# Modulation columns with 64 moving columns in place of one, and refitted order constants, in an adaLN attention and MLP block

## The chip, the cores and the metric

The kernel runs on one core of one Trainium2 chip. The metric is the device time of one execution in microseconds (us). Every time is that of the slowest core, here the only one. A single core has no die to be compared with, so a run counts as fast unless it is over 1.5% above the fastest of its kernel.

The engines are called by the names of the profile: PE is TensorE, PEld its weight loads, DVE is VectorE, ACT is ScalarE, POOL is GpSimd. SP is SyncE, which here only issues DMA transfers, one after the other, in a fixed order.

## The reference, cut to what matters

```python
B, S, D, H = 1, 2048, 640, 32          # Dh = 20, F = 1536, all bf16
mod = (silu(c) @ w_mod).reshape(1, 6, 1, 640)
sa, ca, ga, sb, cb, gb = ...           # six rows of 640
h = layernorm(x) * (1 + ca) + sa
q, k, v = heads(h @ wqkv)
x = x + ga * (softmax(q @ k.T * Dh**-0.5) @ v) @ wo
h = layernorm(x) * (1 + cb) + sb
x = x + gb * ((h @ w_gate) * (h @ w_up)) @ w_down
```

Four of the six modulation vectors (sa, ca, sb, cb) are needed as columns, with the 640 features on partitions. The kernel makes them with thin matmuls: a 128x128 block of w_mod is the stationary operand, and one column of silu(c) is the moving one. They are 25 matmuls to a vector, 100 in all. Two vectors are made at the start, two between 76 and 83 us.

## The kernel before

A scheduler in the kernel file simulates all engines when the kernel is built. It writes out one fixed order of instructions for each engine. It has a model of TensorE's clock, with a constant of 3413.3 ns (HAM_W), and where that model asks for it, it puts in "fillers" (identity matmuls of 512 columns). So each constant below changes the order of instructions and not the clock itself. Of the clock: from the first clock record (6.11 us in before) to the end of the span it is 1.00 but for two stretches at 0.50, of 3.41 and 10.24 us in before. The two starts lie 20 times 3.41 us apart in before. A window is below such a stretch of 3.41 us, at either clock.

```python
STEAL_GAP = 300.0       # ScalarE may take over VectorE's copies before 60 us if it is idle this long
HAM_W = 3413.3
CHUNKS = [(0, 512), (512, 512), (1024, 512), (1536, 256), (1792, 256)]   # query columns
QUADS = [(1, 2, 2, 3, 2, 3, 2, 3), 3, 3, (1, 1, 2, 1, 1, 1, 1, 1), (1, 1, 1, 1, 1, 0, 0, 0)]
```

The work of attention goes through 5 chunks of queries times 8 items (one item is 4 heads). ScalarE makes most exponentials. A "quad" is four 512-column units whose exponential VectorE approximates with shifted terms; QUADS says how many quads each item has. A tuple lists the eight items of a chunk, a number stands for all eight.

The column round:

```python
C512, C320, C128, C1 = 216.0, 136.0, 57.0, 26.0        # ns in the scheduler's model

def col_round(v, slot, prio, plus):
    dm, buf = d_wm[v]
    mms = []
    for nbk in range(KD):                               # KD = 5 blocks of 128
        for k in range(KD):
            f = lambda e, b, nbk=nbk, k=k: e.matmul(
                ps[:, b, nbk:nbk + 1], buf[:, k, nbk * 128:(nbk + 1) * 128],
                scol[:, k:k + 1], start=(k == 0), stop=(k == KD - 1))
            mms.append((C1, f))
    # ... then one VectorE copy of ps[:, b, 0:KD] to mcol[:, slot, :]
```

K and Q take a way through DRAM: TensorE makes them, VectorE or ScalarE copies them to the buffer KPA, SyncE writes them to k_rows and q_rows, and SyncE loads them again in the layout that the scores need. All these transfers stand in SyncE's one queue.

The softmax here doesn't subtract the row's maximum and nothing guards it: scores larger than these inputs give would overflow.

## Time and profile before

| | before |
|---|---|
| time, median of 3 runs | 869.32 us (866.98 to 870.48) |
| profiled execution | 867.68 us, span of the trace 865.9 us |
| mean granted clock | 0.992 |
| last exponential on ScalarE ends | 829.00 us |

The first row of the page gives the busy time of each engine, its share of the span and its count of instructions. Lower on the page, one row gives the shares of the chain of work that ended last.

```profile
PE 829.4 (96%) x13568; PEld 327.5 (38%) x13568; DVE 713.1 (82%) x1338; ACT 802.5 (93%) x718; POOL 32.0 (4%) x65
...
PE 44%; ACT 34%; DVE 15%; issue 3%; DMA 2%; POOL 1%; SPq 1%; DVEq 0%; ACTq 0%
```

TensorE and ScalarE are both nearly full, and the chain passes back and forth between them. A shares row like this cannot tell what a change in one stage is worth. This is the timeline of SyncE before (start, length, queue, line, operation, destination and source, count), which I read only afterwards:

```profile
79.53 5.06 SPq L970 DMA_DIRECT2D KT<-k_rows  x8
84.64 0.42 SPq L957 DMA_DIRECT2D k_rows<-KPA  x1
85.20 0.34 SPq L979 DMA_DIRECT2D QT<-q_rows  x1
```

The load of QT for item 2 is issued at 85.20 us, behind eight KT loads. The semaphore that tells of its landing has its last increment at 87.88 us. The score matmuls that need it start at 89.22 us:

```profile
88.30 0.98 PE L747 MATMUL ps_all<-wmb,SCb 128*32 128x320 bf16 x24
89.22 0.60 PE L1180 MATMUL ps_all<-QT,KT 32*128 32x512 bf16 x6
```

The trace shows no wait there, because TensorE came late after three windows at half clock (0.50 from 77.80 to 88.04 us).

### The profile page before, as it was taken

The numbers are of one execution on the slowest core, as the hardware profiler recorded it, in microseconds if no ns is written. First come the engines' busy times: TensorE is split into PE (matmuls) and PEld (weight loads), VectorE is DVE, ScalarE is ACT, GpSimd is POOL, SyncE is SP. The second block draws the span as 40 slices with busy tenths as digits, with TensorE's granted clock in tenths as the row PEclk, the third lists the DMA queues.
The fourth block names the chain that finished last, engine by engine and source line by source line (L and its number), as shares of the span: only waits on it lengthen the run. The fifth ranks groups of instructions, "written<-read, shape, count | busy, mean of one in ns | idle before, by whom it ended". The sixth has DMA issues, their size and how long they took to land.

```text
span 865.9 us, 30616 instructions
## 1 busy us (share of the span) xinstructions
PE 829.4 (96%) x13568; PEld 327.5 (38%) x13568; DVE 713.1 (82%) x1338; ACT 802.5 (93%) x718; POOL 32.0 (4%) x65
## 2 busy tenths in 40 slices
PE   8899999999999999999999999999999999999998
PEld 4433333322233322233333322223445444455577
DVE  7865888796999999999889999999779877775463
ACT  4698999999999999899999999999999999999931
POOL 2300000000001000000000100000001100000000
PEclk9997999999999999999999999999999999999999
DMA  9163331122510125110301011110310036203640
GB/s 300 38 216 94 92 86 37 29 71 76 156 29 23 33 55 146 43 24 6 66 10 44 5 36 44 44 36 2 67 50 7 21 75 139 59 21 82 136 88 18
DMA packets 118459, 56.37 MB, mean 65 GB/s; under 512 B 84439, under 2 KB 118327, under 8 KB 118327
## 3 DMA queue, kind: packets, MB, share of 16 engines
q1 hardware_dynamic: 117399, 53.26, 24.2%
q8 instruction: 107, 1.75, 0.9%
q10 hardware_dynamic: 928, 1.15, 0.4%
q14 instruction: 25, 0.20, 0.1%
HBM read 42.93 MB, written 9.16 MB: 60 GB/s over the span
## 4 chain that ended last, share of the span: by engine, by line
PE 44%; ACT 34%; DVE 15%; issue 3%; DMA 2%; POOL 1%; SPq 1%; DVEq 0%; ACTq 0%
ACT PP L1214 34%; PE ps_all L747 16%; PE ps_all L1596 13%; PE ps_all L1180 12%; DVE DB L1238 4%; DVE DSS L1252 3%; PE ps_all L914 2%; DVE st L802 1%; DMA k_rows<-KPA 1%; DVE st L1400 1%; DVE xck L1390 1%; DVE OT L1305 1%; DVE xn L1407 1%; PE ps_all L829 1%; DMA stg<-in_B_w_gate_dram 1%
## 5 line engine op out<-in xcount | busy, mean ns | idle before, releaser
L1214 ACT ACTIVATE PP<-ps_all 128x1536 bf16<-128x1536 f32 (+1 forms) x691 | 788.3, 1279 | 13.5 <-PE ps_all L1180 9.7
L1180 PE MATMUL ps_all<-QT,KT 32*128 32x512 bf16 (+1 forms) x2560 | 295.2, 341 | 14.5 <-ACT PP L1214 11.5
L1252 DVE TENSOR_SCALAR DSS<-DB 128x2048 int16<-128x2048 int16 x400 | 265.9, 683 | 20.0 <-PE ps_all L1596 17.7
L1238 DVE TENSOR_SCALAR DB<-ps_all 128x512 int16<-128x512 f32 x320 | 217.2, 682 | 38.7 <-PE ps_all L1180 37.0
L1180 PEld LDWEIGHTS ps_all<-QT,KT 32*128 32x128 bf16 x2560 | 77.2, 91 | 256.6 <-ACT PP L1214 185.7
L1596 PE MATMUL ps_all<-PP,Vf 128*32 128x512 bf16 (+3 forms) x2184 | 171.9, 344 | 1.5 <-DVE OT L1305 1.5
L1596 PE MATMUL ps_all<-DSS,Vf 128*32 128x512 bf16 (+2 forms) x1880 | 151.7, 351 | 0.0
L747 PE MATMUL ps_all<-h2T,stg 128*32 128x512 bf16 x1440 | 109.7, 381 | 2.8 <-DVE DB L1238 1.7
L1596 PEld LDWEIGHTS ps_all<-PP,Vf 128*32 128x32 bf16 (+1 forms) x2184 | 48.3, 94 | 95.3 <-issue 84.9
L1596 PEld LDWEIGHTS ps_all<-DSS,Vf 128*32 128x32 bf16 (+1 forms) x1880 | 47.8, 96 | 36.1 <-issue 16.0
L747 PE MATMUL ps_all<-wd,hprod 128*32 128x320 bf16 x1152 | 55.2, 300 | 0.4 <-DVE DB L1238 0.3
L747 PEld LDWEIGHTS ps_all<-h2T,stg 128*32 128x32 bf16 x1440 | 34.8, 96 | 35.1 <-issue 9.4
L1465 DVE CAST gsb<-ps_all 128x512 bf16<-128x512 f32 (+1 forms) x48 | 29.5, 615 | 10.8 <-PE ps_all L747 10.6
L747 PEld LDWEIGHTS ps_all<-wd,hprod 128*32 128x32 bf16 x1152 | 29.2, 96 | 14.9 <-issue 4.8
L747 PE MATMUL ps_all<-wV,hT 128*32 128x320 bf16 x640 | 32.9, 300 | 1.9 <-DVE DB L1238 0.8
L1403 POOL TENSOR_SCALAR sd<-mv 128x1 f32<-128x1 f32 x14 | 7.0, 499 | 739.7 <-DVE mv L1402 739.7
L747 PE MATMUL ps_all<-wo,Ocp 128*32 128x320 bf16 x640 | 31.9, 300 | 0.4 <-DVE xck L1390 0.3
L1596 PE MATMUL ps_all<-DB,Vf 128*32 128x512 bf16 (+2 forms) x376 | 32.1, 349 | 0.0
L1305 DVE STREAM_TRANSPOSE OT<-ps_all 128x512 f32<-128x512 f32 (+1 forms) x40 | 24.2, 605 | 8.8 <-PE ps_all L1596 8.6
L914 PE MATMUL ps_all<-hT,wk 128*32 128x512 bf16 x380 | 29.9, 381 | 0.4 <-DVE Vf L994 0.4
L914 PE MATMUL ps_all<-hT,wq 128*32 128x512 bf16 x375 | 29.0, 394 | 0.9 <-DVE Vf L994 0.3
L1476 DVE TENSOR_TENSOR hprod<-ps_all,gsb 128x512 bf16<-128x512 f32 x36 | 24.5, 681 | 5.3 <-PE ps_all L747 5.3
(107 smaller groups left out, 486.6 us busy)
## 6 DMA issues: line engine op xcount, KB each, us to landing
stg<-in_B_w_gate_dram SPq DMA_DIRECT2D x50, 160.0 KB
stg<-in_B_w_up_dram SPq DMA_DIRECT2D x50, 160.0 KB
KT<-k_rows SPq DMA_DIRECT2D x120, 32.0 KB
QT<-q_rows SPq DMA_DIRECT2D x22, 128.0 KB
wm<-in_w_mod_dram SPq DMA_DIRECT2D x3, 800.0 KB
k_rows<-KPA SPq DMA_DIRECT2D x18, 128.0 KB
x<-in_A_x_dram SPq DMA_DIRECT2D x7, 320.0 KB
xck<-in_A_x_dram SPq DMA_DIRECT2D x3, 640.0 KB
```

The lines of the kernel that those rows point to most:

```text
L747: return lambda e, b: e.matmul(ps[32 * x:32 * x + 32, b, 0:n], lhs()[:, 32 * x:32 * x + 32], rhs(), tile_position=(0, 32 * x), start=st, s ...
L802: bns.append(dve(393, lambda e, t=t, i=i, hf=hf: e.bn_stats(st[:, i, 6 * hf:6 * hf + 6], x0[:, t, 320 * hf:320 * hf + 320]), [d_x[tc][i // ...
L829: f = lambda e, b, i=i, k=k: e.transpose(bankh(b)[:, i * 128:(i + 1) * 128], xn[:, s2, i, k * 128:(k + 1) * 128], ident[:])
L914: f = [lambda e, b_, k=k, x=x: e.matmul(ps[x:x + min(32, w - x), b_, :], wx[:, k, r0 + x:r0 + min(x + 32, w)], hT[tc][:, k, :], tile_posit ...
L1180: ems.append(lambda e, i=i, kt=kt: e.matmul(dstf()[:, i * u.n:(i + 1) * u.n], KT[32 * u.s:32 * u.s + 32, u.j, kt * 128:(kt + 1) * 128], QT ...
L1214: return e.activation(PPs[g % 2][:, cellp["p"], 0:nu * 512], ps[:, b0:b0 + nu, :].rearrange("p b c -> p (b c)"), AFT.Exp, scale=ESCALE)
L1238: return e.tensor_scalar(DB0[:, st_["slot"], x * 512:(x + 1) * 512], bank(cell["b"]), EBIAS, 0.0, op0=ALU.add, op1=ALU.max)
L1252: return e.tensor_scalar(DSS[:, cell["s"], :], DB0[:, st_["slot"], :], float(SHIFTS[jj]), None, op0=ALU.add)
L1305: t1 = Task("dve", n * 1.1 + 70, lambda e: e.transpose(OT[:, 0:n], ps[:, BPV, 0:n]), [], prio=0.0, name=f"T1.{it}")
L1465: f = lambda e: e.tensor_copy(gsb[:, gs, 0:n], ps[:, r.b["b"], 0:n])
L1476: f = lambda e: e.tensor_tensor(hprod[:, fc, 0:n], ps[:, r.b["b"], 0:n], gsb[:, gs, 0:n], ALU.mult)
L1596: ems.append(lambda e, i=i, kt=kt, stt=stt, stp=stp: e.matmul(ps[32 * s:32 * s + mc, BPV, 0:u.n], Vf[:, (kt * H + 4 * u.j + s) * VW:(kt * ...
```

## The change

The intent: each thin matmul takes the same column of silu(c) repeated 64 times as its moving operand, so that TensorE has more work where its clock had fallen to 0.50 (77.80 to 88.04 us of before), at little cost in time. The scheduler's model is told so, it drops fillers, and the constants of the order are chosen anew. The whole of it:

```diff
-STEAL_GAP = 300.0
+STEAL_GAP = 200.0
-QUADS = [(1, 2, 2, 3, 2, 3, 2, 3), 3, 3, (1, 1, 2, 1, 1, 1, 1, 1), (1, 1, 1, 1, 1, 0, 0, 0)]
+QUADS = [(1, 2, 2, 3, 3, 3, 3, 3), 3, 3, 1, (1, 0, 1, 0, 1, 0, 1, 0)]
-    C512, C320, C128, C1 = 216.0, 136.0, 57.0, 26.0
+    C512, C320, C128, C1 = 216.0, 136.0, 57.0, 28.0
+    NCOL = 64
-                f = lambda ...: e.matmul(ps[:, b, nbk:nbk + 1], buf[:, k, nbk * 128:(nbk + 1) * 128],
-                                         scol[:, k:k + 1], ...)
+                f = lambda ...: e.matmul(ps[:, b, nbk * NCOL:nbk * NCOL + NCOL],
+                                         buf[:, k, nbk * 128:(nbk + 1) * 128],
+                                         scol[:, k:k + 1].to_broadcast([128, NCOL]), ...)
+        def src(r):        # the copies read one column of each 64
+            return ps[:, r.b["b"], 0:KD * NCOL].rearrange("p (a b) -> p a b", b=NCOL)[:, :, 0]
-            sc.activity(start, 1.0 if cand.name[:3] == "col" else cand.dur * 2.37)
+            sc.activity(start, cand.dur * 2.37)
```

There are 80 quads before and after. Chunk 0 has two more (items 4 and 6), chunks 3 and 4 have one less each. The fillers in the order go from 48 to 36.

More of the change, by code (lines that the diff above doesn't have):

```diff
@@ L760, in col_round @@
             for k in range(KD):
-                f = lambda e, b, nbk=nbk, k=k: e.matmul(ps[:, b, nbk:nbk + 1], buf[:, k, nbk * 128:(nbk + 1) * 128],
-                                                        scol[:, k:k + 1], start=(k == 0), stop=(k == KD - 1))
+                f = lambda e, b, nbk=nbk, k=k: e.matmul(ps[:, b, nbk * NCOL:nbk * NCOL + NCOL],
+                                                        buf[:, k, nbk * 128:(nbk + 1) * 128],
+                                                        scol[:, k:k + 1].to_broadcast([128, NCOL]),
+                                                        start=(k == 0), stop=(k == KD - 1))
                 mms.append((C1, f))
+        def src(r):
+            return ps[:, r.b["b"], 0:KD * NCOL].rearrange("p (a b) -> p a b", b=NCOL)[:, :, 0]
         def after(r):
             if plus:
-                f = lambda e: e.tensor_scalar(mcol[:, slot, :], ps[:, r.b["b"], 0:KD], 1.0, None, op0=ALU.add)
+                f = lambda e: e.tensor_scalar(mcol[:, slot, :], src(r), 1.0, None, op0=ALU.add)
             else:
-                f = lambda e: e.tensor_copy(mcol[:, slot, :], ps[:, r.b["b"], 0:KD])
+                f = lambda e: e.tensor_copy(mcol[:, slot, :], src(r))
             return [dve(75, f, [r.last], prio=0)]
```

## The prediction

> **What bounds the kernel now.** I read the page first: TensorE is 96% busy and ScalarE 93%, and the chain that ended last is shared between them (PE 44%, ACT 34%). Then the table of busy time by stretches, to see which of the two binds where:
>
> ```profile
> 80.00:90.00 10.00, 10.00 (x135) 3.90 (x136) 1.65 (x6) 6.21 (x6) 0.00 (x0) 0.60 0.46 112
> ...
> 100.00:150.00 50.00, 48.04 (x698) 15.96 (x694) 42.12 (x73) 49.91 (x46) 0.00 (x0) 1.00 0.26 67
> ```
>
> Columns: PE, PEld, DVE, ACT, POOL busy, then granted clock, DMA share, GB/s. From 90 us on ScalarE (the exponentials, L1214) is busy all the time: it binds until its last exponential at 829 us, with TensorE close behind; after it TensorE alone finishes in 34 us. In 80-90 us ScalarE works only 6.21 of 10 us and the granted clock is 0.60. So the page's row of PEclk is next; it has two dips, at the start and here:
>
> ```profile
> PEclk9997999999999999999999999999999999999999
> ```
>
> Finer stretches put the edges of half clock at 9.52 to 12.93 us and 77.80 to 88.04 us: one and three times 3.41 us, and the two starts are 20 times 3.41 us apart. So the clock is decided on a fixed grid of 3.41 us. On that grid:
>
> ```profile
> 74.39:77.80 3.41, 2.10 (x37) 0.94 (x34) 1.89 (x3) 2.60 (x3) 0.00 (x0) 1.00 0.24 62
> 77.80:81.21 3.41, 3.41 (x38) 1.02 (x37) 0.69 (x1) 2.38 (x2) 0.00 (x0) 0.50 0.50 119
> 81.21:84.63 3.42, 3.42 (x46) 1.38 (x43) 0.33 (x2) 2.46 (x3) 0.00 (x0) 0.50 0.44 105
> 84.63:88.04 3.41, 3.41 (x33) 0.95 (x33) 0.69 (x1) 2.34 (x2) 0.00 (x0) 0.50 0.39 107
> 88.04:91.45 3.41, 3.19 (x57) 1.32 (x49) 2.04 (x4) 1.93 (x3) 0.00 (x0) 1.00 0.30 80
> ```
>
> The timeline of TensorE shows what stood in the window before the drop, and in the next ones: the modulation columns (L761, one moving column each) and an idle gap of 1.31 us.
>
> ```profile
> 75.59 0.40 PE L914 MATMUL ps_all<-hT,wk 128*32 128x512 bf16 x4
> 75.92 0.48 PE L761 MATMUL ps_all<-scol,wm 128*128 128x1 bf16 x13
> 77.71 0.58 PE L1180 MATMUL ps_all<-QT,KT 32*128 32x512 bf16 x3 [1.31 <-ACT PP L1214]
> ...
> 80.72 0.61 PE L761 MATMUL ps_all<-scol,wm 128*128 128x1 bf16 x17
> 81.26 0.61 PE L1180 MATMUL ps_all<-QT,KT 32*128 32x512 bf16 x3
> 81.80 0.66 PE L761 MATMUL ps_all<-scol,wm 128*128 128x1 bf16 x19
> ```
>
> The gap is put down to the exponential, which ended at 76.99. But in the instruction order that score matmul also waits for four loads of KT, whose issue ends at 76.92: I take it for a DMA wait. It is there in the changed order too.
>
> [...] 25 matmuls took 0.78 us and one lasts 165 ns, so (780-165)/24 = 25.6 ns from start to start. For 64 columns no run here shows it[...].
>
> **How thin.** I count activity as moving columns times the share of the array in use, so 128 for each 32-row or 32-column matmul of 512 columns (an assumption of mine). Four of the filler matmuls of 512 columns took 1.02 us, the last 0.38, so 0.215 us each: a full window holds 3.41/0.215 x 512, or 8,130. The window from 74.39 has 18 quarter matmuls (2,304), 13 for the columns and some 80 of the next score: 2,400, and the clock fell. The next two have 2,620 and 2,530, and it stayed down. The fourth has 3,200, and it rose. At the start, 6.11 to 9.52 has four fillers and 37 single columns: 2,085, down; 9.52 to 12.93 has one filler, 20 transposes of 128 columns and 13 single ones: 3,085, up. [...]
>
> **The change part by part.**
> - Columns: 100 matmuls of 1 column become 64. [...] The results lie 64 apart in the bank; 5 x 64 = 320 columns fit, and the two kinds of copy, 156 to 160 ns for five elements, stay.
> - Activity: 12 of them stand before the gap in the new order, so 12 x 64 = 768 in place of 13. The window from 74.39 comes to about 3,150[...]. The drop at 77.8 us should go. At the start, 6.11 to 9.52 holds some 36 x 64 = 2,300[...], as the new order has no fillers between the two rounds: that dip stays.
> - Worth of the drop: in 77.80 to 91.45 ScalarE works 2.38 + 2.46 + 2.34 + 1.93 = 9.11 of 13.65 us, so 4.54 idle. About 0.5 of it is the end of the wait for KT, which stays. The other 4.0 are TensorE at half speed and its backlog. As ScalarE binds right after, nearly all is gained: **-3.9 us**. (From TensorE: 10.24 us at half clock are 5.1 us of lost work, an upper limit.)
> - Fillers: 48 become 36 in the order. They run only where TensorE had nothing else: 0.
> - Refitted quads: 80 quads (four 512-column units whose exponential VectorE makes) stay 80; two move into items 4 and 6 of chunk 0, one out of chunk 3 and one out of chunk 4. ScalarE: 788.3 us over 1,728 units is 0.456 us a unit, so -3.65 us in chunk 0, +1.8 in chunk 3 and in chunk 4. VectorE, for a quad: 4 x 682 (L1238) + 5 x 683 ns (L1252) = 6.1 us. TensorE: 24 matmuls in place of 4, five passes of four more, 5 x 0.215 = 1.08 us a quad. In the stretch of the late items of chunk 0:
>
> ```profile
> 130.00:232.00 102.00, 98.94 (x1310) 30.52 (x1307) 83.99 (x141) 101.99 (x91) 0.00 (x0) 1.00 0.23 65
> 232.00:425.00 193.00, 187.02 (x2497) 59.70 (x2497) 182.56 (x321) 189.70 (x168) 5.09 (x8) 1.00 0.22 53
> ```
>
> VectorE has 18 us free there and takes 12.3, reaching the 94% that it already has in chunk 1 (second line). But TensorE has 3 us free and takes 2.2. So of the 3.65 us I count 1.5 to 2. Chunk 3 gives back 1.8 (ScalarE 114.54 of 115 us). In chunk 4 both are full (705 to 830 us: TensorE 122.93, ScalarE 123.86 of 125), and ScalarE has 34 idle us at the end, so the 1.08 us less of TensorE count there. Sum: about **-0.7 us**.
> - The shorter gap for work that ScalarE takes over from VectorE before 60 us: the counts of every form on ScalarE and VectorE are the same in both orders, so 0.
>
> Sum: +0.3 - 3.9 - 0.7 = -4.3 us. From the median of 869.3 that is 865.0; from the profiled execution (867.68) it is 863.4. I put it at **864.4 us**.
>
> **The rivals.**
> 1. The gap, not the columns, throttles, so the dip stays. For it: the gap is 1.31 us and remains[...]. Against it: the next two windows had TensorE busy throughout and still failed; in them thin columns stood in the way. Time: 868 to 869.
> 2. The wait for KT takes the dip's place: a faster TensorE meets the same loads[...] (in the chain, k_rows writes of 4.04 and KT loads of 2.61 us stand before 70 us). I have left 0.5 us; if it takes 2 more, 866.5.
> 3. VectorE or TensorE becomes the bound of chunk 0 by the two quads: TensorE at 98.94 of 102 us speaks for it, VectorE's 18 us against. Then chunk 3's 1.8 us are lost without a gain: 866 to 867.
> 4. The refit does all that it intends (3.65 us in chunk 0, a shorter tail): 861.
>
> **Range and chances.** The four stand within 861 to 869. The timed runs of before spread by 3.5 us[...]. I take 861 to 868. 2% is 17.4 us, over three times the whole loss by the clock in that stage, so faster by over 2% is nearly out of the question, and nothing added costs 17 us: chances 0.02 faster, 0.97 the same, 0.01 slower.
>
> **What would show it.** Granted clock 1.0 from 13 us to the end, no dip at 78 to 88; the one at 9.5 to 13 still there. ScalarE over 9 us busy in 80 to 90 (6.21 before). [...] The end of chunk 0 (the eighth transposition of PV sums, 238.48 us before) some 5 us earlier, of which 4 by 95 us; then part given back over chunk 3. VectorE near 94% in 130 to 230. It is wrong if the dip stays, if another appears in later windows where fillers were dropped (1.7 us each at half clock), or if the first stage's gain is gone by 600 us.

## More of the kernel before

The two loads matter later (cut):

```python
kt_ready[(j, tc)] = [dma("sp", 32 * 1024, lambda ...: e.dma_start(
    KT[32*s:32*s+32, j, tc*512:(tc+1)*512], KS[...]), dps, prio=1.4, dur=450.0) for s in range(4)]
qt_ready[(j, ci)] = [dma("sp", 128 * n * 2, lambda ...: e.dma_start(
    QT[ci][:, j, :], QS[...]), [...], prio=1.6, dur=450.0)]
# the score matmuls of item j of chunk ci wait for qt_ready[(j, ci)] and kt_ready[(j, tc)]
```

## The result, and the profile after

| | before | after |
|---|---|---|
| median, 4 runs each, same chip | 869.82 us (866.98 to 870.48) | 872.45 us (872.21 to 872.81) |
| profiled execution | 867.68 us | 872.21 us |
| span of the trace | 865.9 us | 870.4 us |
| mean granted clock | 0.992 | 0.994 |
| last exponential ends | 829.00 us | 834.25 us |

The ratio is 1.0037, with a 95% interval of 1.0014 to 1.006. A ratio is here always the mean time of one kernel's fast runs over the mean of the other's of the same rounds, so it is not quite the ratio of the medians. Within 2% the two kernels are the same, as foretold, but the time lies some 8 us above the predicted 864.4 and outside its range. The change lost about 3 us where it was to gain over 4.

The profiled execution of before is one of its faster ones, some 2 us under its median. So of the 4.5 us between the two spans about 2 are that execution's luck.

The page of after: busy times, the granted clock in 40 slices, and the shares of the chain.

```profile
PE 830.1 (95%) x13516; PEld 328.2 (38%) x13516; DVE 711.7 (82%) x1338; ACT 804.3 (92%) x718; POOL 30.4 (3%) x65
...
PEclk9999899999999999999999999999999999999999
...
PE 49%; ACT 24%; DVE 16%; SPq 4%; DMA 3%; issue 3%; POOL 1%; DVEq 0%; ACTq 0%
```

The 7 in the fourth slice is gone, but an 8 stands in the fifth. And SPq, SyncE issuing transfers, has grown from 1% of the chain to 4%. Now the stage itself, as busy time by stretches. Each row has the stretch and its length, then PE, PEld, DVE, ACT and POOL with counts, then granted clock, DMA share and GB/s. First before, for the whole stage:

```profile
76.00:95.00 19.00, 17.32 (x224) 6.32 (x228) 8.36 (x18) 13.65 (x13) 0.00 (x0) 0.73 0.44 102
```

Then after, with the stretch of 80 to 90 us and the late items of chunk 0 that the prediction shows of before:

```profile
76.00:95.00 19.00, 13.94 (x200) 5.88 (x200) 7.65 (x14) 13.57 (x12) 0.00 (x0) 0.90 0.35 85
80.00:90.00 10.00, 6.37 (x111) 3.03 (x107) 1.49 (x4) 5.65 (x6) 0.00 (x0) 1.00 0.44 102
91.20:98.05 6.85, 6.85 (x74) 2.04 (x64) 4.09 (x9) 5.00 (x5) 0.00 (x0) 0.51 0.53 136
130.00:232.00 102.00, 98.33 (x1336) 31.15 (x1328) 94.68 (x161) 100.35 (x89) 0.00 (x0) 1.00 0.22 63
```

In 80 to 90 us the clock rose from 0.60 to 1.00, so the drop is gone. But ScalarE works 5.65 us there, where it had 6.21 and was to have over 9, and TensorE is now busy for 6.37 us in place of 10.00. TensorE got faster and then stood still. Half clock comes back from 91.3 to 98.1 us, two windows long. Over the whole stage ScalarE has 13.57 us of work done, against 13.65: nothing was gained.

What TensorE stood still for is in its timeline (start, length, engine, line, operation, names, shapes, count, and in brackets the idle time before it and what ended it):

```profile
84.78 0.85 PE L747 MATMUL ps_all<-wmb,SCb 128*32 128x320 bf16 x20
85.46 0.39 PE L1602 MATMUL ps_all<-PP,Vf 128*32 128x512 bf16 x4
89.48 0.71 PE L1186 MATMUL ps_all<-QT,KT 32*128 32x512 bf16 x7 [3.63 <-DMA QT<-q_rows]
```

It waits 3.63 us for the QT load of item 2. The score starts at 89.48 us, hardly later than the 89.22 us of before. The chain of after, in order of time, shows where that load stood:

```profile
85.13 1.20 SPq L976
...
86.38 0.41 SPq L976
86.79 0.05 issue
86.84 0.42 SPq L963
...
87.40 2.04 DMA QT<-q_rows
89.44 0.05 issue
89.48 0.63 PE ps_all L1186 x6
```

SyncE issues one transfer after another: KT loads (L976), a k_rows write (L963), then QT, which lands 2.04 us after its issue. SyncE ran almost without a pause from 65.4 to 87.7 us, over 22 us; its longest pause in the listed part of the chain is 0.44 us. Its queue shows the eight KT loads again:

```profile
80.84 5.95 SPq L976 DMA_DIRECT2D KT<-k_rows  x8
86.84 0.42 SPq L963 DMA_DIRECT2D k_rows<-KPA  x1
87.40 0.34 SPq L985 DMA_DIRECT2D QT<-q_rows  x1
```

The median of the 120 KT issues is 0.42 us in both kernels, the longest 1.73 us before and 1.66 after; in the chain above, one of the eight takes 1.20 us. In 65.4 to 87.7 us the DMA engines have a share of only 0.34: the queue was the limit, not the transfers. In before it was as full, from 64.4 to 85.5 us.

The rest of the loss comes late. The end of item 3 (the fourth, as items count from 0) is marked by the transposition of its PV sums, the softmax weights times V. The last exponentials end 829.00 us (799.18 + 29.82) before and 834.25 us (798.77 + 35.48) after. Before:

```profile
141.10 0.71 DVE L1305 STREAM_TRANSPOSE OT<-ps_all 128x512 f32<-128x512 f32 x1
...
799.18 29.82 ACT L1214 ACTIVATE PP<-ps_all 128x1024 bf16<-128x1024 f32 x26
```

After:

```profile
143.67 0.72 DVE L1311 STREAM_TRANSPOSE OT<-ps_all 128x512 f32<-128x512 f32 x1 [0.24 <-PE ps_all L1602]
...
798.77 35.48 ACT L1220 ACTIVATE PP<-ps_all 128x1536 bf16<-128x1536 f32 x31
```

From item 3 to the last exponential it is 687.9 us before and 690.6 us after. From item 3 to the end of the span it is 724.8 and 726.7. Counting from item 3 is useful, because executions of one order differ before it and hardly after it (the early QT of the experiments lies before item 3 and is not counted as another order). To the last exponential, the five profiles with the order of before have 687.9 to 688.0 us, the three with the order of after 690.6 to 690.7. To the end of the span, the three have 726.7, 726.8 and 726.7, and four of the five 724.8, 725.3, 723.8 and 724.0 (a mean of 724.5): the part after the last exponential differs from one execution to the next, 35.8 to 37.4 us in the order of before. So from item 3 the new order loses 2.7 us to the last exponential, and about 2.2 us to the end.

### The profile page after: what moved, and what is told of

Same layout as the page of the kernel before. It is cut to its first block, busy times and chain, and to the rows that moved or that the text cites. A ratio compares the mean times of both kernels' runs of the same rounds, so it can differ in the third digit from the quotient of the medians.

```text
span 870.4 us, 30503 instructions
## 1 busy us (share of the span) xinstructions
PE 830.1 (95%) x13516; PEld 328.2 (38%) x13516; DVE 711.7 (82%) x1338; ACT 804.3 (92%) x718; POOL 30.4 (3%) x65
## 4 chain that ended last, share of the span: by engine, by line
PE 49%; ACT 24%; DVE 16%; SPq 4%; DMA 3%; issue 3%; POOL 1%; DVEq 0%; ACTq 0%
ACT PP L1220 24%; PE ps_all L747 16%; PE ps_all L1602 15%; PE ps_all L1186 14%; DVE DB L1244 5%; DVE DSS L1258 4%; PE ps_all L920 3%; SPq L976 2%; DMA k_rows<-KPA 2%; DVE st L808 1%; DMA wm<-in_w_mod_dram 1%; SPq L1330 1%; DVE OT L1311 1%; DMA xck<-in_A_x_dram 1%; DVE h2T L1429 1%
## 5 line engine op out<-in xcount | busy, mean ns | idle before, releaser
L747 PE MATMUL ps_all<-h2T,stg 128*32 128x512 bf16 x1440 | 112.3, 381 | 2.9 <-DVE DB L1244 0.9
L747 PE MATMUL ps_all<-wd,hprod 128*32 128x320 bf16 x1152 | 54.8, 300 | 0.9 <-DVE DB L1244 0.3
```

The lines of the kernel that those rows point to most:

```text
L747: return lambda e, b: e.matmul(ps[32 * x:32 * x + 32, b, 0:n], lhs()[:, 32 * x:32 * x + 32], rhs(), tile_position=(0, 32 * x), start=st, s ...
```

## The experiments

The theory after the result: (a) in the stage of 76 to 95 us the half clock and the wait for QT cover each other, so that removing only one gains nothing; (b) the refitted quads cost some 2 us later; (c) the 64 columns themselves cost next to nothing. The rivals: the broadcast columns are slow; the clock is what binds and the new half-clock stretch is the loss; or the wait for QT alone binds and half clock is without worth.

### order_after_1col: the order of after with one column

```diff
-    NCOL = 64
+    NCOL = 1
```

> The changed kernel with every instruction in the same place, only the column matmuls back to one moving column. Theory (the wait for the load of QT set by the SyncE queue hides the half clock): the dip at about 78 to 88 us comes back, the score that waits for QT starts at 89 to 90 us all the same (89.48 in the changed kernel), and the time stays within 1.5 us of the changed kernel's 872.4. Rival (the 64 columns do save the half-clock stage, and the new order loses it elsewhere): without them the kernel gets 3 to 5 us slower, 875 to 877.

Measured: median 871.12 us against 868.97 for before on the same chip, ratio 1.0031 (1.0017 to 1.0045). With one column or 64, the order is as slow. The new order makes the loss, not the columns. TensorE waits for QT again:

```profile
88.23 0.71 PE L1186 MATMUL ps_all<-QT,KT 32*128 32x512 bf16 x7 [3.87 <-DMA QT<-q_rows]
```

Against what I expected, the clock held at 77.8 us even with single columns in this execution, and fell from 89.3 to 96.2 us. Its mean clock over the six runs was 0.991, under the 0.9935 of after, and yet it was not slower. So the drop at 77.8 us is not what makes this order slow. That half clock costs nothing here isn't shown by this: it stands behind the wait in both kernels.

### order_before_64col: the order of before with 64 columns

```diff
-STEAL_GAP = 200.0 / QUADS new / C1 = 28.0 / activity: cand.dur * 2.37
+STEAL_GAP = 300.0 / QUADS old / C1 = 26.0 / activity: 1.0 for columns
     NCOL = 64        # kept: the order is that of before, the matmuls are those of after
```

> The kernel before with every instruction in the same place, only the column matmuls with 64 moving columns. Theory: no dip at 78 to 88 us, but the score at 89.2 us waits for QT (issued at 85 to 87 us by SyncE), so ScalarE gains at most 1 to 2 us by 95 us, and the time is within 2 us of the kernel before. If the prediction's step was right by itself, 3.9 us are gained: about 866.

Measured: 869.03 us against 868.97, ratio 0.9997 (0.9982 to 1.0012). Columns alone, in the old order, neither gain nor cost. The drop at 77.8 us is gone, and in its place is a wait for QT, issued at 86.97 us:

```profile
89.03 1.03 PE L1186 MATMUL ps_all<-QT,KT 32*128 32x512 bf16 x6 [4.06 <-DMA QT<-q_rows]
```

The score that started at 89.22 us, after three windows at half clock, starts at 89.03 us, after matmuls at full clock and a wait. This is the plainest case of the two covering each other: the instructions stand in the same order, the matmuls before the score finished 4 us earlier, and the score did not. Half clock then came from 88.1 to 98.3 us, three windows that begin while TensorE stands idle. The same 10.24 us at half clock as in before were there, only behind the start of the score and no longer ahead of it.

### columns_alone: the columns and their order, old quads

```diff
-STEAL_GAP = 200.0
-QUADS = [(1, 2, 2, 3, 3, 3, 3, 3), 3, 3, 1, (1, 0, 1, 0, 1, 0, 1, 0)]
+STEAL_GAP = 300.0
+QUADS = [(1, 2, 2, 3, 2, 3, 2, 3), 3, 3, (1, 1, 2, 1, 1, 1, 1, 1), (1, 1, 1, 1, 1, 0, 0, 0)]
```

> 64 columns and their new weight in the order's bookkeeping, with the old numbers of quads and the old gap. Theory that the QT wait ate the gain: no dip at 78 us, a TensorE gap of 3 us or more before the QT score, a dip after it, 869 to 872. Theory that the refit of quads is the loss: 865 to 867.

Measured: 869.35 us, ratio 1.0003 (0.9989 to 1.0017). TensorE waits 3.29 us for QT and starts the score at 87.65 us. Half clock stood at 8.4 to 11.9 and at 86.9 to 97.2 us. The part that was to bring 3.9 us brings none.

### refit_alone: the new quads in the kernel before

```diff
-STEAL_GAP = 300.0
-QUADS = [(1, 2, 2, 3, 2, 3, 2, 3), 3, 3, (1, 1, 2, 1, 1, 1, 1, 1), (1, 1, 1, 1, 1, 0, 0, 0)]
+STEAL_GAP = 200.0
+QUADS = [(1, 2, 2, 3, 3, 3, 3, 3), 3, 3, 1, (1, 0, 1, 0, 1, 0, 1, 0)]
```

> The kernel before with the new numbers of quads and the new gap, columns of 1. If the refit is neutral, as both chunks are bound by ScalarE and the total of its work is the same: within 1 us of before, with the dip at 78 us. If the refit is the loss: 872 to 874. By the prediction's sum: 0.7 us faster.

Measured: 868.89 us, ratio 1.0000 (0.9986 to 1.0014). The refit alone costs nothing that the runs can show, which my theory had not foretold in that form. From item 3 to the end its one profile has 725.05 us, 0.5 more than the mean of before. The last exponential tells more, as it repeats so well: from item 3 it comes 1.3 us later here than in before (689.2 against 687.9), 0.6 us later in the two profiles with the order of columns_alone (688.5), and 2.7 us later with both (690.6). So the parts do not add: 1.0003 and 1.0000 alone, 1.0037 together. Each part makes the scheduler emit another order for most of the kernel.

The profile has another lesson. With single columns, the clock did not fall at 78 us in this execution (the score of 77.39 us has an idle gap of 0.72 us before it, where before has 1.31), and TensorE waited 3.20 us for QT as the others did. One window at half clock followed, from 90.2 to 93.6 us.

### after_qt_early: the QT load of item 2 ahead of four KT loads

The disputed wait itself, taken away by an earlier load. The whole edit changes the order of SyncE's queue alone: the load is put before the fifth of the eight KT loads.

```diff
+    at_ = next(k for k, t in enumerate(sc.all) if t.name == "QT2.0")
+    kts = [k for k in range(at_) if sc.all[k].name == "KT"][-8:]
+    sc.all.insert(kts[4], sc.all.pop(at_))
```

> The changed kernel; on SyncE the load of QT set 2 stands four KT loads and one write earlier, all else in place. Theory (the wait for this load takes the gain): the score waits under 1 us for it in place of 3.6 us, its start comes from 89.5 to about 86 us, the dip at 91 us goes, and the time falls by 3 to 5 us, to 867.5 to 869.5. Rival (the loss lies in the refitted quads after 140 us and the early stage is made up anyway): within 1 us of the changed kernel's 872.

Measured: 866.07 us against 870.58, ratio 0.9958 (0.994 to 0.9977), below the 867.5 to 869.5 that I expected. Moving one DMA issue turns a loss of 0.4% into a gain of 0.4%. The queue of SyncE:

```profile
78.43 2.93 SPq L976 DMA_DIRECT2D KT<-k_rows  x4
81.49 0.35 SPq L985 DMA_DIRECT2D QT<-q_rows  x1
82.28 2.66 SPq L976 DMA_DIRECT2D KT<-k_rows  x4
```

TensorE starts the score without a wait:

```profile
83.80 0.46 PE L1187 MATMUL ps_all<-QT,KT 32*128 32x512 bf16 x4
```

There is no half clock after the first 6.8 us of this execution, and no wait of a matmul of over a microsecond in the stage. (The mean clock is 1.0 because it counts the time before the first clock record as full. It was not: nine fillers took 4.02 us at the start here, 0.43 us apart, where four at full clock took 1.02.) ScalarE in the stage:

```profile
76.00:95.00 19.00, 17.68 (x281) 7.35 (x281) 12.49 (x27) 18.13 (x17) 0.00 (x0) 1.00 0.40 100
```

It works 18.13 us in place of 13.57: this is about the 4.5 us of idle time that the prediction had counted there, 3.9 of them as gained with the clock. Item 3 ends at 135.81 us, and from there to the end it is again 726.7 us, as in after. The loss of the late order stays.

### before_qt_early: the same load moved in the kernel before

The edit is the same one, made in the kernel before, with its single columns and old quads.

> The kernel before with the same move of the QT load, columns of 1. If half clock and the QT wait cover each other: where the clock drops at 78 us, TensorE gets to this score late anyway, and the gain is 0 to 1 us; in executions without that drop it is more. Time 866 to 869. Rival (the QT load alone binds): 865, as with 64 columns.

Measured: 864.21 us against 870.58, ratio 0.9941 (0.9925 to 0.9957). My theory expected little, because half clock would hold the score where the wait had. The rival, that the QT load alone binds, came true. The clocks of the runs give part of the reason: in four of the six the clock fell seldom or not at all, with single columns. These four had a granted clock of 0.996 to 1.0 and 864.0 to 864.2 us; two had 0.994 and 866.0 and 866.4 us. The profiled one had 1.0, though it ran at half clock up to its first clock record at 13.9 us, which this mean doesn't count. One half-clock window of 3.41 us takes 0.002 off the mean clock (half of 3.41 in 866). So one to three more windows at half clock go with some 2 us, where the prediction had 3.9 for three. That the two slower runs are still some 4 us under before is more than a perfect cover would allow; no profile shows those two. The wait in the profiled run is nearly gone:

```profile
86.80 0.60 PE L1181 MATMUL ps_all<-QT,KT 32*128 32x512 bf16 x6 [0.80 <-DMA QT<-q_rows]
```

### before_64col_qt_early and columns_qt_early: are the columns worth anything once the load is early?

The first is order_before_64col, the second columns_alone, each with the edit above and nothing else.

> The kernel before with 64 columns and the QT load moved: both covers taken away. Theory: no dip from 76 to 98 us, ScalarE over 16 of the 19 us from 76 to 95, time 3 to 4 us under the kernel before, 865 to 866. If another load takes the place of QT at once (rival): 868 to 869, with a TensorE wait on KT or another QT between 85 and 100 us.

> 64 columns with their own order, old quads, QT load moved. Theory: as the kernel before with both, 865 to 866. Rival: 868 to 869.

Measured: 865.37 us, ratio 0.9946 (0.993 to 0.9963), and 865.15 us, ratio 0.9947 (0.9928 to 0.9966). All six runs of before_64col_qt_early had a clock of 0.998 or 1.0, where those with single columns had 0.994 to 1.0; so with QT early the clock held better with the 64 columns in this order. (Of columns_qt_early one run still has 0.994.) They don't shorten the time: with single columns in the same order it was 0.9941, inside the other's interval. The early load gives about 5 us in either order of the old quads, and the columns add nothing that these runs can show.

### after_qt_early_q81 and after_qt_early_q82: the quads given back

Both are after_qt_early. The first restores chunk 4 alone (81 quads), the second chunks 3 and 4 (82 quads).

```diff
-QUADS = [(1, 2, 2, 3, 3, 3, 3, 3), 3, 3, 1, (1, 0, 1, 0, 1, 0, 1, 0)]
+QUADS = [(1, 2, 2, 3, 3, 3, 3, 3), 3, 3, 1, (1, 1, 1, 1, 1, 0, 0, 0)]                            # q81
+QUADS = [(1, 2, 2, 3, 3, 3, 3, 3), 3, 3, (1, 1, 2, 1, 1, 1, 1, 1), (1, 1, 1, 1, 1, 0, 0, 0)]     # q82
```

> The same with only chunk 4 as before (five quads in place of four, 81 in all). Theory: 1.8 us off the last exponential against the changed kernel with QT moved, time 864. Prediction's step: 1.1 us slower than it, 867.

> The changed kernel with the QT load moved, and chunks 3 and 4 with the quads of the kernel before (82 quads in all: the two more in chunk 0 stay). Theory (ScalarE binds to its last exponential in every chunk, so a quad taken out of chunk 3 or 4 costs its 1.8 us in full): last exponential 3 to 4 us before that of the changed kernel with QT moved (826.4 us), time 862 to 863.5. Prediction's step (TensorE is full in chunk 4, so fewer quads help): no gain or a loss, 866 or more.

Measured: 865.42 us, ratio 0.9955 (0.9936 to 0.9973), and 868.68 us, ratio 0.9987 (0.996 to 1.0014), against 869.10 for before. By the medians neither is better than after_qt_early (0.9958), and the expected 862 to 863.5 of q82 were missed. The profiles tell more, counted from item 3, in us:

| kernel | last exponential | end of the span | from the one to the other |
|---|---|---|---|
| after_qt_early | 690.6 | 726.7 | 36.1 |
| after_qt_early_q81 | 688.1 | 725.1 | 37.0 |
| after_qt_early_q82 | 686.5 | 725.95 | 39.4 |

Giving chunk 4 its quad back brings the last exponential 2.5 us forward and the end 1.6 us. So the quad taken out of chunk 4 makes ScalarE end later; it was predicted to save 1.08 us. That the whole kernel is slower for it isn't shown: the ratios are alike, and 1.6 us is what the ends of two executions of one order can differ by. Giving chunk 3 its quad back as well brings the last exponential forward by 1.6 us more, but the end comes 0.85 us later: 39.4 us after the last exponential is more than any profile with fewer quads has. The likely reason, argued and not tested, is TensorE, which has 40 matmuls of 256 columns more for a quad of chunk 3 or 4 (of the PV matmuls 1,584 have 256 columns in before and 1,504 in after, with two such quads fewer). Why q82 spread so widely (865.09 to 872.64) stays open.

### before_qt_early_q82: more quads in chunk 0 and nothing taken out

This is before_qt_early with the first tuple of the new quads and the rest old. I expected it to be the fastest.

> The kernel before with the QT load moved and only the two more quads in chunk 0 (82). Theory: chunk 0 gives about 2 us of the 3.65 (as between the kernels before and refitted) and nothing is given back: 862 to 863, the fastest of all. Rival (VectorE or TensorE of chunk 0 is full): 864 as without them.

Measured: 866.2 us, ratio 0.9961 (0.9939 to 0.9982), slower by its median than before_qt_early, not faster. From item 3, ScalarE ends 1.6 us earlier than there (686.4 against 687.95) and TensorE's part after the last exponential is 2.8 us longer (38.6 against 35.8). The profile shows half clock in this stage with QT early, which no other profile does: from 79.3 to 86.1 us, two windows in place of before's three. QT is issued at 82.75 us, lands at 84.84, and nobody waits for it; the score of item 2 starts at 87.47 us, and ScalarE is busy for 15.42 us of the stage (13.65 before, 16.88 in before_qt_early at full clock). So half clock does hold this score by itself, but by less than three windows and a late queue did.

### qt_early_wo_late: less for SyncE to issue ahead of the load

Five loads of the output weights, 2.0 us of issuing near 58 to 60 us, are moved behind the KT loads in before_qt_early; they are needed much later.

```diff
+    late_wo = [t for t in sc.all if t.name == "WO"]
+    sc.all = [t for t in sc.all if t.name != "WO"]
+    # ... put in again after the fourth KT load behind QT2.0
```

> The kernel before with the QT load moved and, besides, five small loads of wo (2.0 us of issue on SyncE at 58 to 60 us) put behind it. Theory that SyncE's issue one after the other is what the stage waits for: the KT and QT loads come 1 to 2 us earlier (KT set at 81.1 and QT at 84.2 us with the QT load moved alone), the waits of 0.8 us each for KT and QT go, and the time is 0.5 to 2 us under that kernel's ratio of 0.9941, so 0.992 to 0.9935 of the kernel before. Rival (after the QT move ScalarE binds there): 0.994 as without it.

Measured: 864.59 us against 869.76, ratio 0.9945 (0.9931 to 0.9959). It is as fast as before_qt_early and no faster, although the KT loads begin at 77.52 us in place of 81.13 and QT at 79.96 in place of 84.17. The wait for QT is gone, and a new one of 1.40 us, for a KT load, stands at 90.39 us. So the gain of an earlier queue is used up, in the medians, after some 5 us. ScalarE in the stage:

```profile
76.00:95.00 19.00, 17.16 (x269) 6.70 (x270) 12.47 (x27) 17.58 (x16) 0.00 (x0) 1.00 0.48 116
```

This is the fastest single execution (862.61 us), and one execution proves nothing. Four kernels, before_qt_early, before_64col_qt_early, columns_qt_early and qt_early_wo_late, are about 5 us under before and cannot be told apart.

### All kernels side by side

Ratios to before on the same chip, and what one profile of each showed, in us: the start of the score of item 2, its wait for QT, how long half clock lasted after that start, the time from it to the transposition of item 3, and ScalarE's busy time in 76 to 95 us.

| kernel | ratio | score starts | wait for QT | half clock after it | from score to item 3 | ScalarE busy |
|---|---|---|---|---|---|---|
| before | 1 | 89.22 | none, half clock before it | 0 | 51.9 | 13.65 |
| after | 1.0037 | 89.48 | 3.63 | 6.8 | 54.2 | 13.57 |
| order_after_1col | 1.0031 | 88.23 | 3.87 | 6.8 | 54.1 | 13.17 |
| order_before_64col | 0.9997 | 89.03 | 4.06 | 9.3 | 54.8 | 12.30 |
| columns_alone | 1.0003 | 87.65 | 3.29 | 9.5 | 54.8 | 12.93 |
| refit_alone | 1.0000 | 88.16 | 3.20 | 3.4 | 52.9 | 14.00 |
| after_qt_early | 0.9958 | 83.80 | none | 0 | 52.0 | 18.13 |
| before_qt_early | 0.9941 | 86.80 | 0.80 | 0 | 51.8 | 16.88 |
| before_64col_qt_early | 0.9946 | 87.93 | 1.01 | 0 | 51.8 | 16.38 |
| columns_qt_early | 0.9947 | 85.79 | 1.66 | 0 | 51.4 | 16.63 |
| after_qt_early_q81 | 0.9955 | 87.18 | none | 0 | 51.6 | 17.34 |
| after_qt_early_q82 | 0.9987 | 85.82 | 1.48 | 0 | 51.5 | 16.80 |
| before_qt_early_q82 | 0.9961 | 87.47 | none, half clock before it | 0 | 52.0 | 15.42 |
| qt_early_wo_late | 0.9945 | 83.48 | none; 1.40 for KT later | 0 | 53.1 | 17.58 |

The rows fall into two groups, by whether QT is late (in the ratios, all but after_qt_early_q82), and not by the number of columns or by whether the clock dropped first.

The table also shows what the waits bring with them. In all five profiles with a wait of over 3 us for QT, half clock stands behind the score, and item 3 comes later by it: 51.4 to 52.0 us after the score with none (53.1 with the wait for KT), 52.9 with one window, 54.1 and 54.2 with two, 54.8 with most of three. So each window there goes with about 1 us. The rival that the new half-clock stretch is the loss was thus right in part: the clock's drop was not removed, it went from before the score to behind it. No run separates the wait from the half clock that follows it, as after_qt_early removes both.

## Why the prediction was wrong

**The bound of the stage.** The reading of the stage was right in that ScalarE starved in 80 to 90 us and that its work was what counted. It was wrong in what starved it. TensorE at half clock was one of two causes: three windows of it held the score of item 2 to 89.22 us in before, and the late QT alone held it to 87.65 to 89.48 us in the five kernels where the clock had not dropped first. The prediction read the waits of before, and a cause that is covered by another shows no wait.

**The drop of the clock (the step that failed).** "As ScalarE binds right after, nearly all is gained: -3.9 us." The first half of the step held: the drop at 77.8 to 88.0 us is gone with the 64 columns, in order_before_64col too, and the count of the prediction foretold that. This count rests on an assumption about what to count, and it is rough: a recount from the traces puts 2,570 to 2,700 into the window before the drop, not 2,400, as a matmul at the edge of a window can be counted to either side. What keeps the clock up was not shown. And two profiles with single columns (order_after_1col, refit_alone) don't have the drop either, so one profile doesn't show that the columns did it; the clocks of the runs with QT early, six of each kind, are the better sign. The gain was 0 (0.9997 in the old order, 1.0003 with its own). In its place stand 3.3 to 4.1 us of waiting for QT in the three kernels with 64 columns, and then two or three windows of half clock again, which put item 3 off by 2 to 3 us more. In after the score came 0.26 us later than in before (89.48 against 89.22), and item 3 another 2.3 us later (54.2 against 51.9 us from the score). The bound for a hidden transfer was there to be read: in before QT lands at 87.88 us, 2.68 us after its issue, so the score of 89.22 could come forward by 1.3 us at most. The sign that the prediction gave, the eighth transposition some 5 us before 238.48 us, failed as well: it came at 241.78 us.

**Rival 2 was the right one, of the wrong size and name.** "The wait for KT takes the dip's place" was sized at up to 2 us, 866.5 in all. The wait was for QT, which stood behind the KT loads in SyncE's queue, and it took, with the half clock behind it, all 3.9. In after the queue also ran later than before, 1.0 us at its start (65.40 against 64.38 us) and 2.2 us at QT (87.40 against 85.20), which the prediction had not looked for. It had counted on "the same loads"; they are issued in a fixed order by an engine that was itself full (in after from 65.40 to 87.74 us).

**The columns, +0.3 us.** The author's estimate; no run before the result had 64 columns. It is not contradicted, but too small for the runs: 0.9997 in the old order, with an interval of 1.3 us to each side. At the start of after one round of 25 took 0.95 us (31.5 ns from start to start, (950 - 193)/24) and the second, at half clock, 1.52 us (53 ns, (1520 - 242)/24); before they took 0.78 us (25.6 ns) and 0.80 us. At full clock 100 x (31.5 - 25.6) ns is 0.6 us, an estimate from these rounds. The expected dip at the start appeared in after as a half-speed round; in this profile the first score comes at 16.94 us, where before had it at 16.57. After:

```profile
7.79 0.95 PE L762 MATMUL ps_all<-scol,wm 128*128 128x64 bf16 x25 [1.63 <-DMA wm<-in_w_mod_dram]
9.34 1.52 PE L762 MATMUL ps_all<-scol,wm 128*128 128x64 bf16 x25 [0.60 <-DMA wm<-in_w_mod_dram]
```

**Fillers and the shorter gap, 0 each.** The gap constant changes no instruction at all. No new dip came where a filler had stood; the new dip at 91.2 us follows the wait for QT and is absent in after_qt_early.

**The refit, -0.7 us.** Wrong in sign where it was applied, in the order of after; for refit_alone the interval of its ratio holds both 0 and -0.7 us. What each chunk takes can be read from the exponentials on ScalarE, counted in order from the end of item 3's to the end of each chunk's (an estimate, as those of two chunks mix a little at the border). From before to after, chunk 0 takes 98.1 and 97.1 us, chunk 1 192.9 and 191.7, chunk 2 190.0 and 191.0, chunk 3 100.9 and 102.6, chunk 4 107.9 and 110.0. So chunks 0 and 1 gain 2.2 us, where 1.5 to 2 were counted for chunk 0, chunk 2 takes 0.9 of it back unforeseen, chunk 3 costs 1.6, near the 1.8 of the prediction, and chunk 4 costs 2.1: a loss of 2.5 us at the last exponential. VectorE is at 94.68 of 102 us in the late items, as expected (93%). The term that was mis-signed is chunk 4: "the 1.08 us less of TensorE count there" assumed that TensorE sets the end. ScalarE sets the last exponential, and the part after it is no shorter without the quad than executions differ by anyway (36.2 us after; 35.8 to 37.4 in the order of before). In after_qt_early_q81, with the quad back, chunk 4 takes 107.8 us again.

**The sum.** In place of -4.3 us, the two profiled executions lie 4.5 us apart: 2.6 up to item 3 (0.3 by the later score, 2.3 behind it, with the half clock) and 1.9 after it. The medians lie only 2.6 us apart, and the means 3.2 us by the ratio, as before's profiled execution is one of its fast ones. No profile shows where its slower ones lose 2 us more, so the loss of the medians can't be split with certainty; the part after item 3, which hardly differs between executions, is some 2.2 us of it.

**What stays open.** The refit alone costs nothing that shows in the time (1.0000), though the same quads cost 2 us together with the columns; from item 3 its one profile shows 1.3 us to the last exponential and 0.5 us to the end. The order of nearly every instruction differs between the two, and no run separates which part of it matters. Also open is the spread of some 2 us between executions of one kernel before item 3 (the first transposition of PV sums already comes at 62.8 to 64.1 us in the fourteen profiles), what sets the length of single DMA issues (0.42 us or up to 1.7), and why the time fell by 4 us in the two slower runs of before_qt_early as well.

## What to carry to other kernels

Before counting a slow stretch as gain, look for the transfers that its consumer needs next and read when they land, although no wait shows: issue plus landing time is the earliest start, and the gain ends there (85.20 + 2.68 us for QT in before, 1.3 us ahead of its score). Half clock can also stand behind a wait that comes to light, as it did here in all five profiles with a wait of over 3 us, about 1 us for each window. A queue of transfers on one engine can be full for 22 us at a DMA share of 0.34, so its order is worth the same care as that of the matmuls; one load moved ahead of four was worth 5 us here, more than the whole change. And where two engines are both near full, a constant fitted in one stage has to be judged by which of them ends the last stage.
